# Loading v by token tiles, with GpSimd copies across the partition halves, in a fused attention and expert kernel

## The chip, the core and the metric

The program runs on one core of a Trainium2 chip. TensorE (PE in the rows; PEld is its weight load) multiplies, VectorE (DVE), ScalarE (ACT) and GpSimd (POOL) work on tiles of 128 partitions, and SyncE (SP) issues most of the DMAs. A row of an engine's name with a q (SPq, POOLq) is that engine's instruction queue. The metric is the device time of one execution in microseconds (us), as the median of several runs.

## The reference, cut to what matters

```python
q_c, k_c, v_c = (a.reshape(B, H, 9, 64, 64) for a in (q, k, v))   # B=8, H=8, S=576 tokens, D=64
scores = np.matmul(q_c, k_c.transpose(0, 1, 2, 4, 3)) / np.sqrt(64)
attn = np.exp(scores - scores.max(-1, keepdims=True))
attn = attn / (attn.sum(-1, keepdims=True) + 1e-09)
x = np.matmul(attn, v_c)               # per chunk of 64 tokens and head
x = x.reshape(B, H, S, D).transpose(0, 2, 1, 3).reshape(4608, 512)
# stage 2: tokens with x @ w_skip > 0 go to the best of 8 experts (512 -> 1024 -> 512), gated, plus x
# stage 3: h = max(x @ w1, x @ w2, x @ w3) (768 wide); out = h @ w_out
```

Attention is local: the 64 tokens of a chunk attend only to each other, in each of 8 heads. All numbers are float32.

## The kernel before, in words

The 4608 tokens are worked on in 36 tiles of 128 tokens, two chunks each. Two tiles form a unit of 256 tokens, for which q and k are loaded together (`load_qk`, L191 to L204), five units ahead of use. A row of 512 bytes holds two neighbouring tokens, so a pair copy (`pair_heads`, L213 to L219) first brings them into shape: on ScalarE for unit 0, on VectorE for unit 1, on GpSimd from unit 2 on. TensorE turns them (`qk_transpose`), ScalarE moves the result to SBUF (qT and kT, L234), and `scores` multiplies them in quarters of the array, 64 by 64: the quarter's rows are the half of the partitions in which a head lies (`par`, 0 or 1, even or odd head), its columns the half that stands for one of the two chunks (`c2`). VectorE takes the maximum and subtracts it (L251, L253), ScalarE takes the exponential, TensorE turns the result, ScalarE copies it to aT (L267), and `values` (L273 to L297) multiplies it with v. A column of ones behind the 64 columns of v gives the sum by which VectorE divides (L293 to L295).

For this product the rows of v must lie in the same half of the partitions as the head's rows of aT. Before, `load_v` (L206 to L211) brings one batch of 576 tokens with eight DMAs, one for each head, each to the 64 partitions of its head's half: token k of a chunk lies in partition k or 64 + k, and the chunks lie side by side. Three such tiles (NV = 3, L173 and L174) hold three batches. Batch 0 is loaded in two parts, behind units 1 and 2 of q and k; batches 1 and 2 follow units 3 and 4; a later batch is loaded when the product has left the one three before it (L586 to L588).

Behind the product come the routing steps: `x_transpose`, `logits`, and for each group of four tiles `route`, `place` and `store_x` (L440 to L445, GpSimd's DMA of 512 tokens to `x_dram`) and, nine tiles behind, `send_id` (L420 to L429, a GpSimd DMA for each tile). The first tile of a group also clears the last columns of the rows for its tokens (a memset on GpSimd, L291), in one of two buffers whose earlier rows must have been stored. From tile 22 on the weights of the first expert are loaded (`load_raw`, L94 to L98) behind the last load issued so far, and split by ScalarE (L90) and VectorE (L91).

The order of TensorE's instructions is that of the program text in this loop (L573 to L635). On the other engines, SP and the DMA queues among them, a planner orders the instructions by its own estimate of when each can run; the chip then runs each engine's instructions in that order. Where one waits, all behind it on that engine wait.

Of the kernel before, what the change touches and what calls it, by code (L numbers as in the profile page):

```python
# [9 lines left out]
F32 = mybir.dt.float32  # L10
# [9 lines left out]
P = 128  # L20
B, H, S, D = 8, 8, 576, 64
# [6 lines left out]
UT = 256  # L28
NU = N // UT
NT = N // P  # L30
# [7 lines left out]
def kernel(  # L38
# [15 lines left out]
    nc = tc.nc  # L54
# [16 lines left out]
    def four_kb(shape, dt, name, aside=False):  # L71
        return bpool.tile(shape, dt, tag="s4" if aside else "b4", name=name, bufs=2 if aside else 4)
# [93 lines left out]
    def two_banks(tag, name):  # L166
        return psum1.tile([P, 2, 512], F32, tag=tag, name=name)

    apool = p1.enter_context(tc.tile_pool(name="apool", bufs=2))
    nc.gpsimd.memset(ids_sb, N)  # L170
    nc.gpsimd.dma_start(ids_dram.rearrange("(p c) o -> p (c o)", p=P), ids_sb)

    NV, CB = 3, S // 64  # L173
    v_all = [apool.tile([P, CB, 4, D + 1], F32, name=f"v_all{i}", bufs=1) for i in range(NV)]  # L174
    for i, t in enumerate(v_all):
        (nc.gpsimd if i else nc.vector).memset(t[:, :, :, D], 1.0)
    none = kpool.tile([1, XW], F32, name="none")
    nc.gpsimd.memset(none, 0.0)
    nc.gpsimd.dma_start(x_dram[N:N + 1, :], none)

    def pieces(u):
        got, t = [], u * UT
        while t < (u + 1) * UT:
            b, s = divmod(t, S)
            n = min((u + 1) * UT - t, S - s)
            got.append((t - u * UT, b, s, n))
            t += n
        return got


    def load_qk(u):  # L191
        if u % 5 < 3:
            qt = four_kb([P, H, 2 * D], F32, f"qt{u}", u % 5 == 2)
            kt = four_kb([P, H, 2 * D], F32, f"kt{u}", u % 5 == 2)
        else:
            both = bpool.tile([P, 2, H, 2 * D], F32, tag="b8", name=f"qkt{u}")
            qt, kt = both[:, 0], both[:, 1]
        for h0, h1 in [(0, 4), (4, 8)] if u == 0 else [(0, 8)]:
            for off, b, s, n in pieces(u):
                pr = slice(off // 2, (off + n) // 2)  # L200
                for dst, src in ((qt, q), (kt, k)):
                    link["load"] = nc.sync.dma_start(
                        dst[pr, h0:h1], src[b, h0:h1, s:s + n, :].rearrange("h (p r) d -> p h (r d)", r=2))
        units[u] = {"qt": qt, "kt": kt}  # L204

    def load_v(b, c0=0, c1=CB):  # L206
        for h in range(H):
            rows = slice(64 * (h % 2), 64 * (h % 2) + 64)
            link["load"] = nc.sync.dma_start(
                v_all[b % NV][rows, c0:c1, h // 2, :D],  # L210
                v[b, h, 64 * c0:64 * c1, :].rearrange("(c k) d -> k c d", k=64))  # L211

    def pair_heads(u, g):  # L213
        un = units[u]
        for nm in ("q", "k"):
            r = apool.tile([P, 2, H // 2, D], F32, tag=nm + "r", name=f"{nm}r{u}_{g}", bufs=3)
            (nc.scalar.copy if u == 0 else nc.gpsimd.tensor_copy if u > 1 else nc.vector.tensor_copy)(
                r, un[nm + "t"][:, 4 * g:4 * g + 4, :].rearrange("p h (r d) -> p r h d", r=2))
            un[nm + "r", g] = r  # L219
# [47 lines left out]
        nc.scalar.copy(aT, tr)  # L267
        un["aT", s] = aT

    def v_of(chunk):  # L270
        return v_all[chunk // CB % NV][:, chunk % CB]

    def values(t):  # L273
        u, s = divmod(t, 2)
        un = units[u]
        xp = two_banks("xp", f"xp{t}")[:, :, :4 * (D + 1)].rearrange("p r (h d) -> p r h d", h=4)
        for hp in range(4):
            for par, c2 in TILES:
                rows, cols = slice(64 * par, 64 * par + 64), slice(64 * c2, 64 * c2 + 64)
                nc.tensor.matmul(  # L280
                    xp[cols, par, hp, :], un["aT", s][rows, hp, cols], v_of(2 * t + c2)[rows, hp, :],
                    start=True, stop=True)
        g, j = PLACE[t]
        if j == 0:
            if g == len(SIZES) - 1:
                parts = [four_kb([P, 1, XW], F32, f"xg{g}_{i}", True) for i in range(SIZES[g])]
            else:
                parts = [bpool.tile([P, GT, XW], F32, tag="xg", name=f"xg{g}")[:, :SIZES[g], :]]
            groups[g] = parts, apool.tile([P, GT, E + 1], F32, tag="lg", name=f"lg{g}")
            for part in parts:  # L290
                nc.gpsimd.memset(part[:, :, DM + 1:], 0.0)  # L291
        sm = apool.tile([P, 2, 4], F32, tag="sm", name=f"sm{t}", bufs=3)
        nc.vector.tensor_scalar_add(sm, xp[:, :, :, D], 1e-9)  # L293
        nc.vector.reciprocal(sm, sm)
        nc.vector.tensor_tensor(  # L295
            rows_of(t)[:, :DM].rearrange("p (h r d) -> p r h d", h=4, r=2), xp[:, :, :, :D],
            sm.unsqueeze(3).to_broadcast([P, 2, 4, D]), op=ALU.mult)  # L297

    def rows_of(t):
        g, j = PLACE[t]  # L300
        part, i = divmod(j, groups[g][0][0].shape[1])
        return groups[g][0][part][:, i, :]
# [240 lines left out]

    AHEAD = 11

    units, xt, groups, slots, picks, xgs, xT, link, put, sent = {}, {}, {}, {}, {}, {}, {}, {}, {}, []
    ids_rows = ids_dram.rearrange("(p c) o -> p (c o)", p=P)

    def in_turn(load, *what):
        with tc.issue_after(link["load"].ins) if "load" in link else nullcontext():  # L550
            load(*what)

    first_v = {1: [(0, 0, 4)], 2: [(0, 4, CB)], 3: [(1,)], 4: [(2,)]}
    def load_gates():
        nc.sync.dma_start(wcat[:, :, :E], w_gate.rearrange("(c p) e -> p c e", p=P))
        link["load"] = nc.sync.dma_start(wcat[:, :, E], w_skip.rearrange("(c p) -> p c", p=P))

    for u in range(5):
        in_turn(load_qk, u)
        for part in first_v.get(u, ()):  # L560
            in_turn(load_v, *part)
        if u == 2:
            in_turn(load_gates)
        if u < 2:
            pair_heads(u, 0)
            pair_heads(u, 1)
            if u == 0:
                qk_transpose(0, 0)
                qk_transpose(0, 1)
# [3 lines left out]
    for t in range(NT + LAG):  # L573
        u, s = divmod(t, 2)
        if s == 0 and u + 5 < NU:
            load_qk(u + 5)
        if u + 2 < NU:
            pair_heads(u + 2, s)
        if t == 8:
# [3 lines left out]
            nc.gpsimd.tensor_copy(col_f, col_i)  # L583
        if 0 <= t - 2 < NT:
            values(t - 2)
        done = (2 * t - 2) // CB - 1  # L586
        if done >= 0 and (2 * t - 4) // CB <= done and done + NV < B:
            load_v(done + NV)  # L588
        if t < NT:
            scores(t)  # L590
        if t % 2 == 0 and 0 <= t - 22 <= 16:
            i = (t - 22) // 2
# [18 lines left out]
        if 0 <= t - 4 < NT:  # L611
            g, j = PLACE[t - 4]
            if j + 1 == SIZES[g]:
# [10 lines left out]
                if g == FIRST:  # L624
# [3 lines left out]
                    rows = START[g + 1] * P  # L628
# [251 lines left out]
    rows = bpool.tile([P, 4, XW], F32, tag="xg", name="xg_0")  # L880
# [165 lines left out]
    for b, (r0, n) in enumerate(BLOCKS):  # L1046
# [31 lines left out]
        for half in range(2):  # L1078
            for i in range(n // P):
# [11 lines left out]
                r = r0 + half * n + i * P  # L1091
# [32 lines left out]
```

## Time and profile before

| | |
|---|---|
| median of 3 runs | 1116.15 us (1113.48 to 1120.66) |
| profiled execution | 1114.1 us |
| its span, from the first to the last instruction | 1112.4 us |
| mean granted TensorE clock | 0.958 of full speed |
| busy: PE, DVE, ACT, POOL | 92%, 51%, 37%, 31% of the span |
| DMA | 217.12 MB, 195 GB/s over the span |

The share of an engine's busy time is over the whole span; a stage can look different. Matmuls overlap each other, so a busy TensorE is not one at its peak. In a timeline row the first number is the start in us from the span's start, the second the time that the instruction (or a run of like ones, xN) took, and the brackets hold the idle time of the engine before it and what ended that. The share of the DMA engines is a mean over 16 engines and can exceed 1, as packets overlap.

### The profile page before, as it was taken

The page shows a single profiled execution, that of the slowest core. Times are in us where ns is not written, and L with a number is a line of the kernel's source. Part 1 is how long each engine was busy: PE and PEld are TensorE (multiplying, and loading weights), DVE is VectorE, ACT ScalarE, POOL GpSimd, SP SyncE. Part 2 cuts the span into 40 slices and gives each one's busy share as a digit, 9 for nine tenths or more (in the row PEclk, how much of TensorE's full clock was granted, in tenths as well). Part 3 has the DMA queues.
Part 4 walks back from the last instruction along what each step waited for, and adds up shares of the span by engine and source line. Part 5 has one row for each costly group of instructions (what it writes and reads, how often), then busy time and mean ns, then how long its engine had stood idle before and what let it go on. Part 6 is the DMA issues. An engine that isn't in the chain of part 4 may idle for free.

```text
span 1112.4 us, 19589 instructions
## 1 busy us (share of the span) xinstructions
PE 1023.5 (92%) x7544; PEld 870.5 (78%) x7544; DVE 570.7 (51%) x1113; ACT 416.5 (37%) x737; POOL 340.8 (31%) x339
## 2 busy tenths in 40 slices
PE   7778879888999997999899799999999999999997
PEld 5667768777878786887687588788888888788996
DVE  3566657666855477351498762335234442443241
ACT  4546557334434335341444242222322232223231
POOL 2254434372432244530432160122312140223021
PEclk8989969698999998999999899999999999999999
DMA  8999983366863548454998734664466545666591
GB/s 197 200 271 222 252 222 117 135 204 231 287 225 118 187 159 284 154 178 144 299 322 287 262 114 139 189 188 118 164 195 188 165 140 167 178 187 207 187 286 38
DMA packets 213616, 217.12 MB, mean 195 GB/s; under 512 B 48779, under 2 KB 177803, under 8 KB 213504
## 3 DMA queue, kind: packets, MB, share of 16 engines
q1 hardware_dynamic: 200320, 174.18, 55.2%
q0 software_dynamic: 10592, 33.20, 8.6%
q10 hardware_dynamic: 2592, 8.26, 2.0%
q8 instruction: 69, 1.13, 0.4%
q14 instruction: 43, 0.35, 0.1%
HBM read 175.15 MB, written 41.83 MB: 195 GB/s over the span
## 4 chain that ended last, share of the span: by engine, by line
PE 41%; DMA 6%; DVE 3%; issue 3%; POOL 1%; ACT 0%; SPq 0%; POOLq 0%; DVEq 0%; ACTq 0%
PE f_a L681 5%; PE f_a L683 5%; PE f_a L682 5%; PE o L681 4%; PE o L682 4%; PE o L683 4%; DMA ws<-m_sums 3%; PE f_d L681 3%; PE f_d L683 3%; PE f_d L682 3%; DMA m_sums<-n_q 2%; PE f_b L681 1%; PE f_b L682 1%; PE f_b L683 1%; PE trf L855 1%
## 5 line engine op out<-in xcount | busy, mean ns | idle before, releaser
L91 POOL TENSOR_TENSOR fh<-best,fh 128x512 fp32r<-128x512 f32 (+1 forms) x60 | 77.1, 1291 | 361.0 <-ACT fh L90 276.2
L681 PE MATMUL f_a<-x_t,ws 128*128 128x512 f32 (+1 forms) x270 | 100.8, 373 | 6.2 <-DVE p L1009 5.5
L682 PE MATMUL f_a<-x_t,ws 128*128 128x512 f32 (+1 forms) x270 | 99.9, 370 | 0.0
L683 PE MATMUL f_a<-x_t,ws 128*128 128x512 f32 (+1 forms) x270 | 99.7, 370 | 0.0
L90 ACT CAST whi_e<-raw_e 128x1024 fp32r<-128x1024 f32 x64 | 66.0, 1048 | 71.7 <-DMA raw_e<-in_moe_w_dram 40.8
L681 PE MATMUL h<-xhi,whi_e 128*128 128x256 f32 x256 | 76.2, 298 | 12.8 <-ACTq L958 7.0
L682 PE MATMUL o<-wlo_m,fh 128*128 128x512 f32 x216 | 84.6, 392 | 0.0
L681 PE MATMUL o<-whi_m,fh 128*128 128x512 f32 x216 | 83.4, 392 | 0.0
L683 PE MATMUL o<-whi_m,fh 128*128 128x512 f32 x216 | 83.4, 392 | 0.0
L682 PE MATMUL h<-xlo,whi_e 128*128 128x256 f32 x256 | 75.2, 294 | 0.1
L683 PE MATMUL h<-xhi,wlo_e 128*128 128x256 f32 x256 | 74.6, 293 | 0.0
L681 PE MATMUL y<-whi_e,hhi 128*128 128x512 f32 x184 | 73.9, 403 | 0.6 <-ACT hhi L748 0.6
L683 PE MATMUL y<-whi_e,hlo 128*128 128x512 f32 x184 | 72.9, 399 | 0.2
L682 PE MATMUL y<-wlo_e,hhi 128*128 128x512 f32 x184 | 72.4, 394 | 0.0
L91 POOL TENSOR_TENSOR wlo_e<-raw_e,whi_e 128x1024 fp32r<-128x1024 f32 x21 | 52.8, 2514 | 50.3 <-ACT whi_e L90 44.1
L90 ACT CAST fh<-best 128x512 fp32r<-128x512 f32 (+1 forms) x60 | 34.7, 579 | 88.6 <-DVE best L1011 57.0
L91 DVE TENSOR_TENSOR wlo_e<-raw_e,whi_e 128x1024 fp32r<-128x1024 f32 x43 | 53.4, 1256 | 27.5 <-ACT whi_e L90 26.2
L681 PEld LDWEIGHTS h<-xhi,whi_e 128*128 128x128 f32 x256 | 51.8, 203 | 15.9 <-ACTq L958 10.4
L681 PEld LDWEIGHTS f_a<-x_t,ws 128*128 128x128 f32 x270 | 51.1, 189 | 15.9 <-DVE p L1009 5.9
L1014 ACT COPY p<-f_a 128x512 f32<-128x512 f32 (+1 forms) x45 | 24.6, 546 | 99.1 <-PE f_a L683 98.9
L683 PEld LDWEIGHTS f_a<-x_t,ws 128*128 128x128 f32 x270 | 51.2, 190 | 8.6
L682 PEld LDWEIGHTS f_a<-x_t,ws 128*128 128x128 f32 x270 | 51.2, 190 | 8.3
(216 smaller groups left out, 2582.7 us busy)
## 6 DMA issues: line engine op xcount, KB each, us to landing
ws<-m_sums SPq DMA_DIRECT2D x135, 512.0 KB, 5.0
raw_e<-in_moe_w_dram SPq DMA_DIRECT2D x64, 512.0 KB, 4.1
ws<-m_sums SPq DMA_DIRECT2D x45, 256.0 KB, 3.9
x<-x_dram SPq DMA_DIRECT2D x36, 256.0 KB, 4.3
out_dram<-os SPq DMA_DIRECT2D x36, 256.0 KB, 2.0
x_dram<-xg POOLq DMA_DIRECT2D x8, 1040.0 KB, 6.9
v_all<-in_v_dram SPq DMA_DIRECT2D x56, 144.0 KB, 5.6
m_sums<-n_raw ACTq DMA_DIRECT2D x18, 448.0 KB, 4.8
```

The lines of the kernel that those rows point to most:

```text
L90: nc.scalar.copy(hi, src),
L91: eng.tensor_tensor(lo, src, hi.bitcast(F32), op=ALU.subtract),
L681: nc.tensor.matmul(acc, ahi, bhi, start=first, stop=False, skip_group_check=onto)
L682: nc.tensor.matmul(acc, ahi, blo, start=False, stop=False, skip_group_check=onto)
L683: return nc.tensor.matmul(acc, alo, bhi, start=False, stop=last, skip_group_check=onto)
L855: nc.tensor.transpose(tr[:, i * P:(i + 1) * P], row[:, c * P:(c + 1) * P], ident)
L1014: nc.scalar.copy(p1, acc_a)
```

## The change

v is loaded by the tile of 128 tokens, one token to a partition, with all eight heads side by side (one DMA, or two where the tile crosses the end of a batch). Eight such tiles are held; the first eight are loaded behind units 1 to 4 of q and k, two at a time, and the tile t + 6 in step t, once the product of tile t - 2 has run. In this layout chunk 0 of a tile lies in partitions 0 to 63 and chunk 1 in 64 to 127, for all heads; the quarters in which the head's half and the chunk's half differ (`par` not equal to `c2`) read v from another tile, `vm`, into which `cross` copies the even heads of the upper half and the odd heads of the lower half, two copies of 64 partitions by 4 x 65 elements for each tile. VectorE makes them for tiles 0 and 1, GpSimd for the others. The matmuls are the same in number and shape. The GpSimd DMA scratch has its default size again.

```diff
-    NV, CB = 3, S // 64
-    v_all = [apool.tile([P, CB, 4, D + 1], F32, name=f"v_all{i}", bufs=1) for i in range(NV)]
+    NV = 8
+    v_all = [apool.tile([P, H, D + 1], F32, name=f"v_all{i}", bufs=1) for i in range(NV)]
     for i, t in enumerate(v_all):
-        (nc.gpsimd if i else nc.vector).memset(t[:, :, :, D], 1.0)
+        (nc.gpsimd if i > 1 else nc.vector).memset(t[:, :, D], 1.0)
...
-    def pieces(u):
-        got, t = [], u * UT
-        while t < (u + 1) * UT:
+    def pieces(t, end):
+        got, t0 = [], t
+        while t < end:
...
-    def load_v(b, c0=0, c1=CB):
-        for h in range(H):
-            rows = slice(64 * (h % 2), 64 * (h % 2) + 64)
+    def load_v(t):
+        for off, b, s, n in pieces(t * P, (t + 1) * P):
             link["load"] = nc.sync.dma_start(
-                v_all[b % NV][rows, c0:c1, h // 2, :D],
-                v[b, h, 64 * c0:64 * c1, :].rearrange("(c k) d -> k c d", k=64))
+                v_all[t % NV][off:off + n, :, :D], v[b, :, s:s + n, :].rearrange("h k d -> k h d"))
+
+    def cross(t):
+        vn = v_all[t % NV].rearrange("p (h r) d -> p r h d", r=2)
+        vm[t] = apool.tile([P, H // 2, D + 1], F32, tag="vm", name=f"vm{t}", bufs=4)
+        eng = nc.vector if t < 2 else nc.gpsimd
+        for par in range(2):
+            to, of = slice(64 * par, 64 * par + 64), slice(64 - 64 * par, 128 - 64 * par)
+            eng.tensor_copy(vm[t][to], vn[of, par])
...
-    def v_of(chunk):
-        return v_all[chunk // CB % NV][:, chunk % CB]
+    def v_of(t, par, c2):
+        return v_all[t % NV].rearrange("p (h r) d -> p r h d", r=2)[:, par] if c2 == par else vm[t]
...
-                    xp[cols, par, hp, :], un["aT", s][rows, hp, cols], v_of(2 * t + c2)[rows, hp, :],
+                    xp[cols, par, hp, :], un["aT", s][rows, hp, cols], v_of(t, par, c2)[rows, hp, :],
...
-    first_v = {1: [(0, 0, 4)], 2: [(0, 4, CB)], 3: [(1,)], 4: [(2,)]}
+    first_v = {1: (0, 1), 2: (2, 3), 3: (4, 5), 4: (6, 7)}
...
         if s == 0 and u + 5 < NU:
             load_qk(u + 5)
+        if t < NT:
+            cross(t)
         if u + 2 < NU:
             pair_heads(u + 2, s)
...
-        done = (2 * t - 2) // CB - 1
-        if done >= 0 and (2 * t - 4) // CB <= done and done + NV < B:
-            load_v(done + NV)
+        if t >= 2 and t - 2 + NV < NT:
+            load_v(t - 2 + NV)
...
-    nc = _bacc.Bacc("TRN2", target_bir_lowering=False, num_devices=1, dynamic_dma_scratch_size=8192)
+    nc = _bacc.Bacc("TRN2", target_bir_lowering=False, num_devices=1)
```

## Rows read from the trace of the kernel before

**Rows 1.** The page, busy time (share of the span) and instructions.
```profile
PE 1023.5 (92%) x7544; PEld 870.5 (78%) x7544; DVE 570.7 (51%) x1113; ACT 416.5 (37%) x737; POOL 340.8 (31%) x339
```

**Rows 2.** Busy time by stretch: length; PE, PEld, DVE, ACT, POOL; clock, DMA share, GB/s.
```profile
60.00:76.00 16.00, 9.69 (x172) 8.83 (x162) 10.23 (x26) 6.16 (x15) 8.79 (x13) 0.79 1.13 275
76.00:136.00 60.00, 54.40 (x1196) 48.98 (x1198) 40.16 (x138) 36.12 (x80) 29.02 (x45) 1.00 1.17 242
136.00:156.00 20.00, 11.86 (x206) 10.82 (x199) 5.83 (x11) 7.87 (x14) 7.59 (x11) 0.66 1.12 252
```

**Rows 3.** Timeline of TensorE: starts of the value products (L280).
```profile
36.80 0.69 PE L280 MATMUL xp<-v_all,aT 64*64 64x65 f32 x30
...
50.37 0.70 PE L280 MATMUL xp<-v_all,aT 64*64 64x65 f32 x32
...
76.22 0.70 PE L280 MATMUL xp<-v_all,aT 64*64 64x65 f32 x32
...
135.38 0.70 PE L280 MATMUL xp<-v_all,aT 64*64 64x65 f32 x32
...
155.17 0.70 PE L280 MATMUL xp<-v_all,aT 64*64 64x65 f32 x32
```

**Rows 4.** TensorE's waits, 0 to 206 us: total, times, longest.
```profile
PE trp L264 <- ACT qT L234: 10.1, 6, 8.1
PE trx L308 <- DVE xg L295: 5.7, 1, 5.7
PE trq L232 <- POOL qr L217: 4.1, 2, 3.2
PE trk L232 <- POOL kr L217: 3.7, 4, 1.4
```

**Rows 5.** Timeline of SP's queue (DMA issues).
```profile
36.40 9.11 SPq L209 DMA_DIRECT2D v_all<-in_v_dram  x8
...
59.03 4.13 SPq L202 DMA_DIRECT2D qkt<-in_k_dram  x1
...
123.36 12.06 SPq L209 DMA_DIRECT2D v_all<-in_v_dram  x8
...
136.27 1.36 SPq L97 DMA_DIRECT2D raw_e<-in_moe_w_dram  x1
```

**Rows 6.** Timeline of GpSimd, TensorE and ScalarE: first work behind a late load.
```profile
42.39 1.17 POOL L217 COPY qr<-qkt 128x512 f32<-128x512 f32 x2 [9.94 <-DMA qkt<-in_q_dram]
...
54.83 0.66 PE L232 MATMUL trk<-ident,kr 128*128 128x128 f32 x4 [1.01 <-POOL kr L217]
...
143.00 1.04 ACT L90 CAST whi_e<-raw_e 128x1024 fp32r<-128x1024 f32 x1 [7.45 <-DMA raw_e<-in_moe_w_dram]
```

**Rows 7.** DMA queue of SP, 39 to 45 us: packets, MB, share.
```profile
q1 hardware_dynamic: 3581, 1.08, 126.3%
```

**Rows 8.** Pair copies by shape on VectorE and GpSimd: busy us, mean ns | idle before.
```profile
L217 DVE COPY qr<-qt 128x512 f32<-128x512 f32 x2 | 0.8, 424 | 3.2 <-DMA qt<-in_q_dram 3.2
...
L217 POOL COPY qr<-qt 128x512 f32<-128x512 f32 x20 | 12.5, 630 | 36.2 <-DMA qt<-in_q_dram 23.7 <-issue 6.9 <-PE trq L232 4.6
```

**Rows 9.** Timeline of GpSimd: id sends, pair copies, a store and a memset.
```profile
61.99 0.99 POOL L422 DMA_INDIRECT ids_dram<-tok_i,rslot  x1 [0.30 <-PE sc L247]
63.29 0.98 POOL L422 DMA_INDIRECT ids_dram<-tok_i,rslot  x1 [0.30 <-PE lp L316]
...
65.54 0.63 POOL L217 COPY qr<-qt 128x512 f32<-128x512 f32 x1
...
68.32 0.60 POOL L217 COPY kr<-kt 128x512 f32<-128x512 f32 x1
...
127.73 0.81 POOL L444 DMA_DIRECT2D x_dram<-xg  x1 [1.48 <-DVE run L352]
134.81 0.12 POOL L291 MEMSET xg<- 128x28 f32 x1 [6.27 <-DMA x_dram<-xg]
```

**Rows 10.** Timeline of VectorE: adds of routing.
```profile
65.58 3.37 DVE L352 TENSOR_TENSOR run<-run,roh 128x8 bf16<-128x8 bf16 x2
```

More of the change, by code (lines that the diff above doesn't have):

```diff
@@ L179 @@
     nc.gpsimd.dma_start(x_dram[N:N + 1, :], none)
-    def pieces(u):
-        got, t = [], u * UT
-        while t < (u + 1) * UT:
+    def pieces(t, end):
+        got, t0 = [], t
+        while t < end:
             b, s = divmod(t, S)
-            n = min((u + 1) * UT - t, S - s)
-            got.append((t - u * UT, b, s, n))
+            n = min(end - t, S - s)
+            got.append((t - t0, b, s, n))
             t += n
@@ L198, in load_qk @@
         for h0, h1 in [(0, 4), (4, 8)] if u == 0 else [(0, 8)]:
-            for off, b, s, n in pieces(u):
+            for off, b, s, n in pieces(u * UT, (u + 1) * UT):
                 pr = slice(off // 2, (off + n) // 2)
@@ L544 @@
     AHEAD = 11
-    units, xt, groups, slots, picks, xgs, xT, link, put, sent = {}, {}, {}, {}, {}, {}, {}, {}, {}, []
+    vm, units, xt, groups, slots, picks, xgs, xT, link, put, sent = {}, {}, {}, {}, {}, {}, {}, {}, {}, {}, []
     ids_rows = ids_dram.rearrange("(p c) o -> p (c o)", p=P)
@@ L560 @@
         for part in first_v.get(u, ()):
-            in_turn(load_v, *part)
+            in_turn(load_v, part)
         if u == 2:
```

## The prediction

> **What bounds the kernel now.** I began with busy time per engine: TensorE is busy 92% of the span [rows 1]. So the time is TensorE's work plus the places where it waits, and the change adds and removes no TensorE instruction. It touches the attention stage alone, roughly the first 204 us. I cut that stage into stretches [rows 2]. From 76 to 136 us TensorE is busy 54.4 of 60 us at a granted clock of 1.00; from 60 to 76 it is busy 9.7 of 16 at 0.79, from 136 to 156 11.9 of 20 at 0.66. The reader is to see two holes here, after each of which the clock falls to between its levels, so that the next tile also runs slower.
>
> The undisturbed pace comes from the starts of the value products [rows 3]: 76.22 to 135.38 us holds 14 tiles, 4.23 us a tile. At that pace two tiles take 8.5 us. From 36.80 to 50.37 two tiles took 13.6 us, 5.1 too many; from 135.38 to 155.17 two took 19.8, 11.3 too many.
>
> Next, what TensorE waited for [rows 4]: 10.1 us for ScalarE's qT, of which one wait is 8.1; 5.7 in one wait for VectorE's xg; 4.1 and 3.7 for the pair copies on GpSimd (longest 3.2 and 1.4). Two of these four lead back to the load queue. SP holds eight v DMAs in a row: 9.11 us at 36.40, 12.06 at 123.36 [rows 5]. Behind the first, the q of unit 4 reached GpSimd only at 42.39, after a 9.94 us wait for its DMA; lateness of the same kind cost TensorE the 1.4 us [rows 4] and 1.01 at 54.83 [rows 6]. Behind the second, the first expert weight was issued only at 136.27 [rows 5], ScalarE stood 7.45 us at its cast [rows 6], and the qT copy queued behind that cast is the 8.1 us wait.
>
> **The change, part by part.**
>
> *Load queue.* 72 v DMAs become 40 (36 tiles; four straddle a batch and need two pieces). Bytes and the 256-byte run stay. With v alone in flight 3,581 packets took 126% of the engines' 6 us [rows 7]; I take that cost per packet as unchanged, so what changes is order: before unit 4's q and k come 1.6 MB of v (six tiles) instead of 2.4 MB (two batches). At 1.08 MB in 6 us [rows 7] the 0.8 MB are 4.4 us, more than the 3.2 us wait. I take the whole 5.1 us excess at 36.80, the 1.4 and the 1.0, and 0.9 of the other 2.2 us of waits for pair copies (7.8 less 3.2, 1.4 and 1.0). The SP cost of one 256 KB v DMA isn't shown: below, 9.11/8 = 1.1 us, above, the 4.13 us of a blocked 512 KB k load [rows 5]; either way SP is never held for 9 to 12 us on end. The load of v for tile t+6 now waits for the product of tile t-2 and for its copies; queued behind it are q, k and the weights, which are needed 8 tiles later or in the MoE stage, and so can bear it.
>
> *First weight.* It is issued after the last v load. That is now one 256 KB DMA instead of eight, so the 12.06 us hold shrinks to about 1 to 4, against a 7.45 us wait. Bounds: nothing gained, or the 11.3 us excess. I take 11.3, since 12.06 less 4.13 is 7.9 and covers the wait. Gains together: 5.1 + 2.4 + 0.9 + 11.3 = 19.7 us.
>
> *VectorE copies of tiles 0 and 1.* Four of 64 x 260. A 128 x 512 copy on VectorE is 0.424 us [rows 8]; by elements per partition 0.22, so 0.9 us in the chain to the first product, with nothing to hide it. Bounds 0 and 1.7 (four full copies); I take 0.9, nearer in shape. More memsets at the start (eight small ones for three) lie beside GpSimd's first wait and I cost them at nothing; without that cover, eight of 0.12 us [rows 9] would be 1.0.
>
> *GpSimd copies of tiles 2 to 35.* 68 of 64 x 260, a form the trace doesn't have, as they also move data to the other 64 partitions. Below: 0.12 us of a memset [rows 9] plus 260/512 of what a 128 x 512 copy takes beyond that, 0.63 - 0.12 [rows 8], gives 0.38. Above: 0.63, a whole copy. I take 0.38, since these copies are the same operation on half as many elements: 3.0 us per four tiles, 26 us in all. Is there room? Per four tiles, 16.9 us, GpSimd is busy 8.2 (29.0 of 60 us [rows 2]). Id sends start 1.30 us apart but last 0.99 [rows 9], adding 1.2 for four. And its queue stands from 128.54 to 134.81 at the memset of the next token rows, which waits 6.27 us for the store of the earlier rows [rows 9]. That is 15.7 of 16.9; with 3.0 more it is 18.7, too much by 1.8 unless copies run inside that wait. They need only v (loaded six tiles ahead) and one of four buffers, so those planned ahead of the memset are hidden; those behind it are what a value product would wait for. I take half hidden and 2 us in all; bounds 0, and with the upper price (5.0 per four tiles, 3.8 too much, six times) 23.
>
> *VectorE beside GpSimd.* At 65.58 two adds of routing took 3.37 us for eight elements a partition each, ending as a run of six GpSimd copies, from 65.54 to 68.92, ran out [rows 9, 10]; xg behind them gave the 5.7 us wait. So an add with both inputs in SBUF stood through the run, not through one copy. Longer runs make this likelier: I take one more, 5.7 us. Bounds: the present one goes (-5.7), or four more (23). The Trainium skill, "SBUF — State Buffer", section "Who interferes with whom", says that such an instruction and a GpSimd instruction that reads SBUF exclude each other until the one that issued first finishes. By that rule alone each collision would cost one copy, 0.6 us, and the sum would be 5 us better; the row shows five times that, and it decides.
>
> *Descriptor scratch.* The kernel's GpSimd DMA scratch goes back to its default. No row shows a DMA issue waiting for it; I cost it at nothing.
>
> **Sum.** -19.7 + 0.9 + 2 + 5.7 = -11.1 us in the attention stage. The MoE stages follow in TensorE's order and start when the routing ends, so I pass it on whole; a planner that orders the later stages otherwise is why the forecast's own range is 6 us either way, a width that I choose. The profiled execution is 1114.1 us (span 1112.4 and 1.7 around it), so 1103.0; the median of the runs is 2.05 higher, hence 1105.0.
>
> **Rivals.**
>
> *GpSimd becomes the bound (slower).* Place: the copies behind the memset that waits for the store. Price: 3.8 us per four tiles over six groups, 23, and two further collisions, 11.4. It decides once GpSimd's work per four tiles passes 16.9 us, which 1.2 us more already does if none of it fits inside the 6.27 us wait. -19.7 + 0.9 + 23 + 11.4 = +15.6: 1132. For it: 15.7 of 16.9 is already taken. Against: the pair copies run several buffers ahead and the wait itself is idle time.
>
> *Copies are free (better).* All of them fall into that wait, and runs get shorter because q and k no longer arrive in a heap: -19.7 + 0.9 = -18.8, 1097; with the present collision gone too, 1092. For it: the burst at 65.54 had queued up behind late loads and id sends. Against: id sends stay, and hold GpSimd 5.2 us at a time.
>
> *The change doesn't reach the late weight.* Packets are as many and as small, so the weight may land as late, and the planner may put the cast as early as before. Then only 8.4 of the 19.7 us come back, and 8.6 are lost: 1116, no change. For it: the DMA share from 76 to 156 us is 1.12 to 1.17 [rows 2], near the 1.26 with v alone [rows 7]. Against: the 12.06 us that SP spent before that weight.
>
> **How the numbers follow.** About 1% (11 us) is what a measurement can tell from no change. Chances: forecast 0.45 (1099 to 1111, its middle on that line), copies free 0.15, weight still late 0.18, GpSimd the bound 0.22. Faster by over 1%: 0.25 of the forecast, 0.15, and 0.02 of the third, 0.42. Slower: 0.18 of the last and 0.03 of the third, 0.21. Within 1%: the remaining 0.37. The range leaves out a tenth at each end: down to 1093, just above copies free with the collision gone, and up to 1130, most of the way to the slower case. The faster cases alone run from 1092 to 1105.
>
> **What would show it.** Right: no stretch of SP beyond 4 us on v; no wait for unit 4's q near 40 us; ScalarE's first weight cast without a wait of several us and the granted clock near 1.00 from 136 to 156; GpSimd copies of 0.3 to 0.4 us. Wrong: value products waiting for the copies, routing adds of several us in more than two places, GpSimd copies above 0.6 us, or a hole of the same length in the MoE stage, which would mean that the gain was given back there.

## The result, and the profile after

The changed kernel took 1132.7 us, the median of four runs, against 1118.41 for four runs of the kernel before beside it: ratio 1.013, 95% interval 1.0086 to 1.0174. It is slower by 14.3 us, where 1105 had been forecast. In two of the five sets of runs below the kernel before took 1136 us, at a lower granted clock, instead of 1115 to 1118, so every ratio in this document is to the kernel before in the same set. The profiled execution has a span of 1128.7 us, 16.3 more than before. The last value product starts at 225.1 us instead of 204.3, so the attention stage ends 20.8 us later, and what follows is 4.5 us shorter (903.6 instead of 908.1).

Line numbers are five or six higher than before. TensorE's stretches, with the columns of [rows 2]:

```profile
17.00:60.00 43.00, 39.46 (x809) 35.84 (x811) 27.15 (x82) 28.25 (x59) 20.50 (x39) 0.96 1.15 229
60.00:76.00 16.00, 13.07 (x266) 11.62 (x260) 9.68 (x25) 8.67 (x18) 7.58 (x15) 0.95 1.02 236
76.00:136.00 60.00, 44.28 (x795) 40.90 (x795) 26.65 (x89) 25.49 (x53) 28.73 (x50) 0.78 0.90 208
136.00:156.00 20.00, 18.14 (x341) 15.98 (x340) 13.27 (x43) 12.10 (x24) 12.12 (x22) 0.83 0.72 199
156.00:204.00 48.00, 34.61 (x573) 30.40 (x575) 27.06 (x86) 23.91 (x48) 30.33 (x50) 0.79 0.46 143
```

Against [rows 2] the holes moved. From 60 to 76 us TensorE is busy 13.07 us instead of 9.69, and from 136 to 156 it is 18.14 instead of 11.86, as the prediction had it. But from 76 to 136, where nothing was to be lost, 54.40 us at a clock of 1.00 became 44.28 at 0.78. Counted in value products, the changed kernel was ahead at 75 us (12.4 tiles of 36 against 10.5) and behind at 135 (21.4 against 23.5) and 195 (30.8 against 34.5). These counts by window come out a half to one and a quarter tiles high by the end of the stage, so differences below a tile are not to be read.

What TensorE waited for, 0 to 230 us (total, times, longest):

```profile
PE trx L313 <- DVE xg L300: 13.0, 4, 6.9
PE trq L237 <- POOL qr L222: 10.7, 5, 4.3
```

The 8.1 us for qT of [rows 4] is gone; the waits for GpSimd's pair copies (4.1 us before) and for VectorE's xg (5.7) have more than doubled. Both lead to GpSimd: xg stood for stores of token rows that GpSimd issues, which it did nowhere before,

```profile
DVE xg L300 <- DMA x_dram<-xg: 14.9, 5, 4.4
```

and TensorE's longest single wait for xg, 6.9 us, is explained below. GpSimd's copies, all of them, with what its queue stood for ahead of them:

```profile
L216 POOL COPY vm<-v_all x68: 394/399/787, 21.2 to 208.6; 64x260 f32<-64x260 f32 x68
its engine sat idle before it (us, times) until:
  DMA ids_dram<-tok_i,rslot: 29.9, 10
  PE trx L313: 14.2, 3
  PE xp L285: 7.8, 2
```

A copy takes 399 ns (the median), as costed. Yet the queue stands 29.9 us, in ten places, until the DMAs of id sends have landed, which have nothing to do with v. It stands a further 31.3 us ahead of copies for TensorE (the two rows above and 4.6, 3.9 and 0.8 us more). In the program, the one thing of TensorE's that a copy waits for is the product of the tile four before, which frees one of the four buffers of `vm`; as TensorE itself was late, part of this is an effect of the loss. A timeline of GpSimd shows how a wait for a send comes about (the bracket is the idle time ahead):

```profile
156.00 1.00 POOL L427 DMA_INDIRECT ids_dram<-tok_i,rslot  x1 [0.16 <-issue]
161.43 0.90 POOL L216 COPY vm<-v_all 64x260 f32<-64x260 f32 x2 [4.43 <-DMA ids_dram<-tok_i,rslot]
162.48 0.99 POOL L427 DMA_INDIRECT ids_dram<-tok_i,rslot  x1 [0.15 <-POOL vm L216]
163.52 0.61 POOL L222 COPY qr<-qkt 128x512 f32<-128x512 f32 x1
```

A send is issued at 156.00, the next copy starts 4.43 us after the send's end, and the next send and the pair copies queue behind it. It is in the compiled program, in GpSimd's order of instructions with the semaphores that each waits for (the sends of lines 65 and 67 count up DMASW3 and DMASW4):

```
65 L427 DMA ids_dram<-tok_i,rslot_890 36864x1 [waits DMASW0_49,DVE_49,Pool_49]
66 L216 COPY vm_1075<-v_all_132 64x260
67 L427 DMA ids_dram<-tok_i,rslot_890 36864x1
...
70 L216 COPY vm_1193<-v_all_133 64x260 [waits DMASW4_49,DMASW3_49,DMAHW0_49,PE_49,Pool_49]
```

18 of the 68 copies wait like this. In the kernel before no copy waits for a send, and the four sends of a group stand one behind the other; here most of them are spread one or two at a time between copies. Late sends have one more customer. VectorE computes the first expert's row numbers ("at") when the sent ids can be loaded:

```profile
174.80 0.69 DVE L258 TENSOR_TENSOR ex<-sc,mx 128x512 f32<-128x512 f32 x1
185.10 0.66 DVE L636 TENSOR_SCALAR at<-ids 128x2 int32<-128x2 int32 x1 [9.61 <-DMA ids<-ids_dram]
185.61 0.15 DVE L298 TENSOR_SCALAR sm<-xp 128x8 f32<-128x8 f32 x1
...
186.95 1.09 PE L313 MATMUL trx<-ident,xg 128*128 128x128 f32 x4 [6.85 <-DVE xg L300]
```

Before, this instruction stood 1.44 us and ran at 172.61, at the same place in VectorE's order. Here it stands 9.61 us with a tile's normalization (sm, xg) behind it. TensorE waits 6.85 us for that xg and is busy 3.12 of the 10 us from 180 to 190 (9.67 before):

```profile
180.00:190.00 10.00, 3.12 (x69) 2.53 (x68) 3.09 (x7) 1.84 (x4) 7.57 (x13) 0.68 0.04 6
```

### The profile page after: what moved, and what is told of

Same layout as the page of the kernel before. It is cut to its first block, busy times and chain, and to the rows that moved or that the text cites. A ratio compares the mean times of both kernels' runs of the same rounds, so it can differ in the third digit from the quotient of the medians.

```text
span 1128.7 us, 19653 instructions
## 1 busy us (share of the span) xinstructions
PE 1032.5 (91%) x7544; PEld 879.0 (78%) x7544; DVE 570.0 (51%) x1118; ACT 418.7 (37%) x737; POOL 363.8 (32%) x411
## 4 chain that ended last, share of the span: by engine, by line
PE 44%; DMA 5%; DVE 1%; issue 0%; ACT 0%; SPq 0%; ACTq 0%; DVEq 0%
PE f_a L687 6%; PE f_a L689 6%; PE f_a L688 6%; PE o L687 4%; PE o L689 4%; PE o L688 4%; DMA ws<-m_sums 4%; PE f_d L687 3%; PE f_d L688 3%; PE f_d L689 3%; PE f_b L689 1%; PE f_b L688 1%; PE f_b L687 1%; PE trf L861 1%; DMA m_sums<-n_q 1%
## 5 line engine op out<-in xcount | busy, mean ns | idle before, releaser
L91 DVE TENSOR_TENSOR wlo_e<-raw_e,whi_e 128x1024 fp32r<-128x1024 f32 x43 | 55.8, 1313 | 23.4 <-ACT whi_e L90 21.4
L687 PEld LDWEIGHTS f_a<-x_t,ws 128*128 128x128 f32 x270 | 51.1, 189 | 16.5 <-DVE p L1015 5.9
L678 POOL DMA_INDIRECT x_dram<-xg,ids_sb x20 | 20.8, 1039 | 115.3 <-DVEq L902 46.9
L689 PEld LDWEIGHTS f_a<-x_t,ws 128*128 128x128 f32 x270 | 51.2, 190 | 8.6
```

The costliest lines, as they stand in the source:

```text
L91: eng.tensor_tensor(lo, src, hi.bitcast(F32), op=ALU.subtract),
L678: ins = nc.gpsimd.indirect_dma_start(out=x_dram[:, :], out_offset=bass.IndirectOffsetOnAxis(ap=ids, axis=0), in_=xg, in_offset=None, bound ...
L687: nc.tensor.matmul(acc, ahi, bhi, start=first, stop=False, skip_group_check=onto)
L689: return nc.tensor.matmul(acc, alo, bhi, start=False, stop=last, skip_group_check=onto)
```

## The experiments

The theories: **A**, the copies' wait for id sends is the loss; **B**, GpSimd's added work is, 68 times 0.40 us; **C**, the new loads cost the time. All medians are in us. A set is a group of runs taken together with the kernel before; there were five. The ratio is to the kernel before in the same set, with its 95% interval, and ratios are compared within a set first. The last two columns are starts, in us, in the profiled execution: of the last value product and of the instruction for "at".

One thing has to be kept in mind where two runs differ by copies: the planner arranges the whole program anew. In the compiled programs of the changed kernel and e1 or e16, of e1 and e2 or e3, of e5 and e6, of e6 and e7, and of the kernel before and e4, the order of the other instructions on VectorE, ScalarE and GpSimd differs too. In e4's, for example, "at" stands behind the softmax of tile 28 and not, as in the kernel before, behind that of tile 29. The difference between two such runs is therefore the price of the copies together with that of the new order, and no run separates these two.

| run | set | median | ratio | interval | last value product | "at" |
|---|---|---|---|---|---|---|
| before (profile of the first run) | | 1118.41 | | | 204.3 | 172.6 |
| changed | | 1132.7 | 1.013 | 1.009 to 1.017 | 225.1 | 185.1 |
| e1 VectorE copies | 1 | 1111.85 | 0.996 | 0.994 to 0.998 | 209.5 | 168.1 |
| e2 same + spare GpSimd copies | 1 | 1126.41 | 1.007 | 1.005 to 1.009 | 221.4 | 175.1 |
| e3 one half each | 1 | 1116.64 | 0.999 | 0.997 to 1.001 | 209.2 | 165.5 |
| e4 before + spare copies | 1 | 1125.03 | 1.006 | 1.004 to 1.008 | 222.0 | 177.3 |
| e5 new order, old layout | 2 | 1124.65 | 1.010 | 1.006 to 1.014 | 218.9 | 180.3 |
| e6 same + spare copies, no id wait | 2 | 1132.01 | 1.016 | 1.012 to 1.020 | 223.0 | 184.8 |
| e7 same, with id wait | 2 | 1156.29 | 1.037 | 1.033 to 1.042 | 252.2 | 208.7 |
| e8 e5 + old scratch size | 2 | 1129.16 | 1.012 | 1.009 to 1.016 | 223.7 | 182.5 |
| e9 before + early weights | 3 | 1138.44 | 1.001 | 0.998 to 1.005 | 223.0 | 185.3 |
| e10 e5 + early weights | 3 | 1122.73 | 0.988 | 0.982 to 0.993 | 221.6 | 178.0 |
| e11 e1, copies later | 3 | 1130.57 | 0.996 | 0.993 to 1.000 | 217.8 | 173.1 |
| e12 e3, copies later | 3 | 1136.87 | 1.000 | 0.997 to 1.004 | 232.9 | 186.2 |
| e13 e10 again | 4 | 1117.98 | 1.002 | 1.000 to 1.004 | 216.7 | 177.5 |
| e14 before, one execution | 4 | 1110.61 | | | 203.5 | 173.5 |
| e15 e9, one execution | 4 | 1115.9 | | | 201.6 | 168.6 |
| e16 ScalarE copies | 4 | 1111.57 | 0.996 | 0.994 to 0.999 | 205.0 | 165.8 |
| e17 changed, "at" on GpSimd | 5 | 1133.69 | 1.000 | 0.996 to 1.004 | 228.4 | 194.6 |
| e18 e16, "at" on GpSimd | 5 | 1126.06 | 0.992 | 0.989 to 0.996 | 216.4 | 174.4 |

**e1, all copies on VectorE.**

```
-        eng = nc.vector if t < 2 else nc.gpsimd
+        eng = nc.vector
```

> The changed kernel with all 72 copies on VectorE (0.291 us each there, against 0.399 us on GpSimd), and nothing else edited. Theory A, the wait: in the changed kernel's program the first copy of a token tile stands on GpSimd until the id sends ahead of it have landed (29.9 us of such waits in the trace, 5.2 the longest), and pair copies, stores and sends queue behind it; VectorE's copies carry no such wait. Then the gains of the new load order stay and little is lost: 1100 us (1094 to 1108), the last value product near 190 us (204.3 before, 225.1 after), no wait of GpSimd for ids_dram. Rival B, too much work on GpSimd: the 68 copies times 0.40 are 27 us of GpSimd's queue; this also gives about 1100 here, and is told apart by the next run. Rival C, the new v loads themselves cost the time: still 1125 to 1135, with the last value product near 225.

No copy waits for an id send now, and the loss is gone; but 1111.85 is only 5 us below the kernel before, not 17. VectorE's busy time shows the price there (count | busy us, mean ns | idle ahead):

```profile
L216 DVE COPY vm<-v_all 64x260 f32<-64x260 f32 x68 | 23.5, 346 | 31.9 <-PE xp L285 15.3 <-DMA v_all<-in_v_dram 13.7 <-issue 1.3
```

23.5 us of work in the 68 copies of this stretch, and VectorE stands 31.9 us ahead of the copies with the softmax of later tiles behind. C, as put (1125 or more), is out.

**e2, the same, and GpSimd as busy as in the changed kernel.** The spare tile is read by nothing.

```
             eng.tensor_copy(vm[t][to], vn[of, par])
+            if t > 1:
+                nc.gpsimd.tensor_copy(spare[t % 2][to], vn[:64, 1])
```

> The kernel with the copies on VectorE, and beside them GpSimd also makes 68 copies of the same 64 x 260 shape from the same v tiles into a spare tile that nothing reads. They wait for the v loads, and not for any id send. Theory A (the wait): GpSimd is as busy as in the changed kernel, yet the time stays within 5 us of the run with VectorE copies alone, 1100 to 1105. Rival B (GpSimd's work): back to 1120 to 1135, with TensorE waiting for pair copies as in the changed kernel (10.7 us). Rival C: 1125 to 1135.

A fell as the whole story: without any wait for an id send, 68 copies of 407 ns on average cost 14.6 us over e1. They are not quite free of waits, though: they stood 8.3 us for v loads.

**e3, half of the copies left on GpSimd**, those that read partitions 0 to 63 and wait for no send.

```
-        for par in range(2):
-            ...
-            eng.tensor_copy(vm[t][to], vn[of, par])
+        nc.vector.tensor_copy(vm[t][:64], vn[64:, 0])
+        eng.tensor_copy(vm[t][64:], vn[:64, 1])
```

> Of each tile's two copies only the one that reads partitions 0 to 63 stays on GpSimd (34 copies), which in the program waits for no id send; the other one goes to VectorE. Theory A: all of the wait is gone, 1098 to 1106, as with VectorE copies alone. Rival B: half of GpSimd's extra work is left, so about half of the loss, 1112 to 1120. Rival C: 1125 to 1135.

1116.64, 4.8 over e1: B's side, and none of GpSimd's copies waits for a send in this program.

**e4, the kernel before with 68 spare copies.**

```
+        if 2 <= t < NT:
+            nc.gpsimd.tensor_copy(tick[t % 2][:64], big[:64, :260])
+            nc.gpsimd.tensor_copy(tick[t % 2][64:], big[:64, :260])
```

> The kernel before, its v loads untouched, with 68 spare copies of 64 x 260 on GpSimd, two per token tile, from a constant tile into a tile that nothing reads; none waits for an id send or a load. Theory A: 68 x 0.40 = 27 us of work that mostly finds GpSimd idle, 1116 to 1121. Rival B: GpSimd has no room for 27 us more, 1126 or above, and the memset behind the store and the pair copies come later. The prediction's own term for these copies alone was 2 us, with 23 as its upper bound.

7.7 us: nearer to B, well above the prediction's 2. These are the only spare copies that wait for nothing. How the work turns into time is only partly seen. The copies ran between 4 and 118 us, but the tiles fell behind after 150 (24.1 done by then against 24.5 in e14's trace of the kernel before, 31.1 against 34.0 by 195), where VectorE stood 6.3 us for the row numbers (now a tile earlier in its order), ScalarE 5.7 for the weight, and the clock was low. So no copy stood in GpSimd's way when the time was lost, and the new order may hold part of the 7.7. e4's stretches:

```profile
170.00:180.00 10.00, 8.18 (x108) 7.58 (x107) 3.56 (x8) 4.60 (x8) 4.81 (x6) 0.77 0.05 7
180.00:190.00 10.00, 8.72 (x143) 7.85 (x144) 6.59 (x22) 6.38 (x13) 5.09 (x8) 0.57 0.38 124
```

and the same of e14:

```profile
170.00:180.00 10.00, 8.80 (x182) 7.88 (x182) 8.17 (x29) 7.17 (x15) 5.18 (x9) 1.00 0.35 109
180.00:190.00 10.00, 9.70 (x183) 9.00 (x183) 7.30 (x19) 6.74 (x13) 6.06 (x7) 0.83 0.45 161
```

TensorE is busy nearly as long and does 251 matmuls instead of 365, at a granted clock of 0.77 and 0.57 instead of 1.00 and 0.83: part of the loss appears as a low clock, whatever brought it down.

**e5, the load order without copies**, v in the layout of the kernel before.

```
+        for c in range(2):
+            b, s = divmod(t * P + 64 * c, S)
+            for par in range(2):
+                link["load"] = nc.sync.dma_start(
+                    v_all[t % NV][64 * par:64 * par + 64, c, :, :D],
+                    v[b, par::2, s:s + 64, :].rearrange("h k d -> k h d"))
...
```

> The load order of the changed kernel without its copies: v still comes one tile of 128 tokens at a time into eight tiles, but each head's 64-token chunk goes straight to the half of the partitions where the products want it, as in the kernel before (four DMAs of 64 KB for a tile in place of one of 256 KB). No copy is left on any engine. Theory L1: the load order is worth what the prediction summed for it, 19.7 us, so 1094 to 1102 and a last value product near 188 us. Rival L2: it is worth little more than the VectorE version showed (1111.9), because a tile of attention still takes TensorE and its producers about 5 us (three tiles in 15 us there, whatever the holes): 1104 to 1112, last value product after 195. Rival L3: the load order itself is worth nothing, 1114 to 1120.

Outside all three: 1124.65, slower than before. At first it runs ahead (22.0 tiles by 120 us against 20.5), then TensorE is busy 2.61 of the 20 us from 136 to 156. SP's and ScalarE's timelines:

```profile
143.03 3.53 SPq L209 DMA_DIRECT2D v_all<-in_v_dram  x4
146.61 0.59 SPq L97 DMA_DIRECT2D raw_e<-in_moe_w_dram  x1
...
151.77 1.04 ACT L90 CAST whi_e<-raw_e 128x1024 fp32r<-128x1024 f32 x1 [21.57 <-DMA raw_e<-in_moe_w_dram]
```

Four 64 KB v DMAs hold SP 3.53 us; 144 of them stand in the queue with everything else, and the first weight is issued ten microseconds later than before. This layout doesn't price the load order alone.

**e6 and e7, e5 with 68 spare GpSimd copies**, from partitions 0 to 63 (no id wait) or across, as in the changed kernel (nine wait for sends).

```
+        if 1 < t < NT:
+            for par in range(2):
+                to, of = slice(64 * par, 64 * par + 64), slice(0, 64)
+                nc.gpsimd.tensor_copy(spare[t % 4][to], v_all[t % NV][of, par])
```

In e7 "of" is slice(64 - 64 * par, 128 - 64 * par).

> The run above, plus 68 copies of 64 x 260 on GpSimd from the v tiles into a spare tile that nothing reads, all from partitions 0 to 63, so that none waits for an id send in the program. Theory A, as revised by the first four runs (GpSimd's added work is the larger part of the loss): 8 to 15 us above the run above, as 68 such copies cost 7.7 us in the kernel before and 14.5 beside VectorE's. Rival (only the waits cost): within 3 us of it.

> The same 68 spare copies, now from the other half of the partitions as in the changed kernel; in the program nine of them wait for id sends that stand just ahead. Theory: the waits add to the work, another 4 to 8 us over the run with copies from partitions 0 to 63, and stores come late (VectorE's xg waits for a store by 10 us or more in all). Rival: within 2 us of it, the waits are idle time.

e6: 7.4 us over e5, as much as in e4. But its copies stood a long time for v loads (GpSimd's waits, 17 to 260 us), and TensorE stood 22.5 us for the pair copies behind them, so this is not the price of the work alone:

```profile
POOL spare L582 <- DMA v_all<-in_v_dram: 44.4, 17, 5.6
```

e7: 24.3 over e6, far more than expected. The same waits in e7:

```profile
POOL spare L582 <- DMA v_all<-in_v_dram: 34.2, 10, 7.4
POOL xg L293 <- DMA x_dram<-xg: 24.3, 4, 8.9
POOL spare L582 <- DMA ids_dram<-tok_i,rslot: 14.9, 7, 3.8
```

The wait for sends is 14.9 us itself and puts the sends and stores behind it later still: the row numbers run at 208.65 instead of 184.81, and the memset of token rows (xg L293) stands 24.3 us for stores (3.9 in e6). The copies stood less for v than in e6, so v doesn't explain it. A is a part, then, and B as well (e2, e4).

**e8, the DMA scratch of the kernel before in e5.**

```
-    nc = _bacc.Bacc("TRN2", target_bir_lowering=False, num_devices=1)
+    nc = _bacc.Bacc("TRN2", target_bir_lowering=False, num_devices=1, dynamic_dma_scratch_size=8192)
```

> The load order without copies, and with the DMA scratch at 8192 bytes a partition as in the kernel before, where the change left the default. The prediction costed that at nothing: within 2 us of the first run of this set. If the larger scratch lets GpSimd's DMAs go earlier, this run is slower by more than that.

4.5 us slower by the medians, with ratios whose intervals overlap. The larger scratch of the change doesn't cost; whether it saves something isn't settled.

**e9, the largest gain alone: the weights' loads four tiles earlier.**

```
-        if t % 2 == 0 and 0 <= t - 22 <= 16:
+        if t % 2 == 0 and 0 <= t - 18 <= 20:
             i = (t - 22) // 2
             with tc.issue_after(link["max"].ins), tc.issue_after(link["exp"].ins):
-                if i < 8:
-                    with tc.issue_after(link["load"].ins):
-                        raws_0[i] = load_raw(*expert_src(0, i))
-                if i:
+                if i > 0:
                     expert_piece(0, i - 1, wpool, raw=raws_0[i - 1])
+                if i + 2 < 8:
+                    with tc.issue_after(link["load"].ins):
+                        raws_0[i + 2] = load_raw(*expert_src(0, i + 2))
```

> The kernel before, its v loads untouched, with the loads of the first expert's weights issued four tiles earlier (two loads further ahead of their casts), so that they stand ahead of the last two v batches in SP's queue. This tries the largest gain of the prediction by itself: 11.3 us for the first weight coming in time. Theory G (the gain is real and keeps): ScalarE's 7.45 us wait for the weight is gone, TensorE's busy time from 136 to 156 us rises from 11.9 to 17 or more, and the time falls to 1102 to 1108. Rival H (given back): the hole goes, but the tiles behind it run no sooner, because the v and q behind the weights come later by the same bytes: 1112 to 1118.

ScalarE no longer waits for the weight, and the ratio is 1.001: the rival.

**e10, the same in e5, and e13, e10 again.**

> The run with v tile by tile in the old layout and no copies (1124.65 us; there the 144 v DMAs took SP 0.88 us each, the first weight was issued only at 146.61 and ScalarE stood 21.57 us for it), with the weights issued earlier in the same way. Theory: that wait is what made this version slow; without it 1100 to 1108, and the load order's gain is shown free of copies. Rival: SP's issue time of the 144 DMAs holds back the q and k loads as well, 1115 or more.

> The version with v tile by tile in the old layout, no copies and the weights issued earlier, once more (ratio 0.988, interval 0.982 to 0.993, on a chip on which the kernel before took 1136 us). If its gain is real and not that chip's, the ratio is 0.983 to 0.993 again; otherwise above 0.995.

0.988 in the third set, 1.002 in the fourth: the gain did not repeat, and in e13's profile ScalarE again stood 8.01 us for the weight. Why one set showed it stays open.

**e14 and e15, the kernel before and e9, one execution of each.**

> The kernel before, unchanged, for a trace from the same chip as the next run. Expected as before: a hole of TensorE of 7 us or more between 136 and 156 us, where ScalarE waits for the first weight, and a last value product near 204 us.

> The kernel before with the weights issued earlier (ratio 1.001, interval 0.998 to 1.005), for a trace from the same chip. It says where the 11.3 us went. Theory H1 (the loads set the pace up to 156 us): no hole at the weight, but no more tiles done by 150 us than in the run of the kernel before, since the DMA engines are as full in both; last value product within 3 us of it. Rival H2: the last value product comes 8 us earlier or more, and the gain is lost behind it, in the start of the expert stage.

e14 settles more than it was meant to. ScalarE's first weight in this execution of the unchanged kernel:

```profile
144.16 1.04 ACT L90 CAST whi_e<-raw_e 128x1024 fp32r<-128x1024 f32 x1 [2.35 <-DMA raw_e<-in_moe_w_dram]
```

and its stretch around it:

```profile
136.00:156.00 20.00, 17.50 (x273) 16.30 (x271) 9.27 (x22) 9.63 (x19) 9.12 (x12) 0.72 1.12 239
```

The wait is 2.35 us, not the 7.45 of [rows 6], TensorE is busy 17.50 us, not 11.86, and still the last value product comes at 203.5 instead of 204.3. This execution stood a tile behind at 135 us (22.5 against 23.5) and level at 150 (24.5 in both): ScalarE's cast starts at nearly the same time, 143.00 and 144.16, and only how long the engines stand ahead of it differs. The hole on which 11.3 us of the prediction rested is there in one execution and hardly in the next, and the tiles end at the same time. e15, with no wait at all: 201.6, within H1's 3 us, though a tile ahead at 150 us (25.5), which H1 had not expected, and no gain in the time.

**e11 and e12, e1 and e3 with the copies one tile later**, just ahead of their products.

```
-        if t < NT:
-            cross(t)
...
+        if 0 <= t - 1 < NT:
+            cross(t - 1)
         if 0 <= t - 2 < NT:
             values(t - 2)
```

> The VectorE version (1111.85 us), each tile's copies put one tile later in the program, just ahead of the products that need them. In that version VectorE's copies stood 15.3 us for TensorE's products to free their buffer and 13.7 us for v, in front of the softmax of later tiles. Theory V (VectorE's queue held the tiles at 5.0 us each): those waits shrink to under 10 us together, 1100 to 1107. Rival: the copies' own 23.5 us on VectorE are the price, and the products now wait for them: 1109 to 1115.

> The version with one half on GpSimd and one on VectorE (1116.64 us), also one tile later. Theory V: 1100 to 1110. Rival (GpSimd's 34 copies cost by their work, 5 us or more over VectorE alone): above the run before it by 4 to 6 us.

Ratios as without the move (0.996 and 1.000), the result that the rivals had named. But V isn't refuted by it: in e11 VectorE's copies still stood 20.0 us for the products and 11.0 for v, so the waits that the move was to shorten were as long as in e1.

**e16, all copies on ScalarE.**

```
-        eng = nc.vector if t < 2 else nc.gpsimd
+        eng = nc.scalar
...
-            eng.tensor_copy(vm[t][to], vn[of, par])
+            eng.copy(vm[t][to], vn[of, par])
```

> The changed kernel with all 72 copies on ScalarE. As with VectorE's (ratio 0.996), no copy waits for an id send and GpSimd has no more to do than before. ScalarE is busy 36 of 60 us from 76 to 136 us in the kernel before; 24 more tiles' copies at about 0.35 us each add 8 or so. Theory (any engine but GpSimd gives a small gain): ratio 0.990 to 1.000. Rival (ScalarE's queue feeds TensorE's transposes, qT and kT, so its copies cost more than VectorE's): 1.000 to 1.015.

0.996, as VectorE's. 410 ns each, 27.9 us for the 68 of this stretch:

```profile
L216 ACT COPY vm<-v_all 64x260 f32<-64x260 f32 x68 | 27.9, 410 | 18.3 <-DMA v_all<-in_v_dram 14.5 <-PE xp L285 2.8
```

So the same loads and copies gain 0.4% from two engines and lose 1.3% from GpSimd.

**e17 and e18, the row numbers on GpSimd** in the changed kernel and in e16.

```
-                    nc.vector.tensor_single_scalar(at, ids_0[:, :2], rows - 1, op=ALU.min)
+                    nc.gpsimd.tensor_single_scalar(at, ids_0[:, :2], rows - 1, op=ALU.min)
```

> The changed kernel with one small instruction moved: the minimum over the first expert's row numbers (128 x 2 integers), for which VectorE stood 9.61 us in the changed kernel and 1.44 in the one before, runs on GpSimd, whose gathers are the only ones to use it. Theory D (the late id sends cost mainly by that stand: VectorE's queue with the softmax of the next tile behind it, TensorE busy 3.12 of 10 us from 180 to 190): 7 to 10 us less than the changed kernel, ratio 1.003 to 1.007, and no 9 us wait on VectorE. Rival P (GpSimd's late copies hold every tile, the stand is one among many): ratio 1.010 to 1.017.

> The ScalarE version (ratio 0.996; VectorE stood 5.17 us for the row numbers there) with the same move. Theory D: 3 to 5 us less, ratio 0.991 to 0.995, the best version so far. Rival P: 0.995 to 1.000, as pair copies on GpSimd now queue behind that wait.

The ratios went D's way: 1.000 (better than D's range) against 1.013, 0.992 against 0.996. But both were compared across sets, and e10 and e13 show that one version's ratio can differ by that much between sets. e17's trace doesn't support D either: the last value product is at 228.4, no earlier than in the changed kernel (in another set), and GpSimd still stands for sends ahead of the copies:

```profile
POOL vm L216 <- DMA ids_dram<-tok_i,rslot: 32.5, 9, 5.4
POOL vm L216 <- DMA v_all<-in_v_dram: 10.9, 5, 6.0
```

What VectorE's stand is worth stays open. Within the fifth set, e18 is 7.6 us below e17: GpSimd is the wrong engine for the copies there too. e1, e16 and e18 are the versions whose intervals lie below the kernel before, by less than 1%; e10 did once, and not when repeated.

## Why the prediction was wrong

- **The failed step is "They need only v (loaded six tiles ahead) and one of four buffers ... I take half hidden and 2 us in all."** The copy's price was right (0.38 forecast, 0.399 measured). What they need was wrong: 18 of 68 also wait for id sends, 29.9 us in all, a wait that no term of the sum has. The wait for one of the four buffers is named and priced at nothing; the copies stood 31.3 us for TensorE to free one. And the hiding was wrong: copies that wait for nothing cost 7.7 us (e4), and those that wait only for v cost 14.6 (e2). With the same loads, the copies on ScalarE instead of GpSimd are 1.7% better (e16), some 19 us, so their place on GpSimd is what made the change slower. How the 19 us divide into the work, the waits for sends and those for buffers isn't shown: the work costs 7.7 to 14.6 us in other kernels, sends to wait for came with 24.3 us in e7, and no run changed the number of buffers.
- **The rival had the total by luck, not the mechanism.** "GpSimd becomes the bound" said 1132, with the copies behind the memset that waits for the store and two further collisions. In the changed kernel no memset stands like that; the copies themselves stand, for sends. And the price was set against 19.7 us of gains that weren't there.
- **The gains, 19.7, were mis-sized.** With the copies on VectorE or ScalarE the whole change gains 4 to 5 us (e1, e16), the copies' own cost there included. *First weight, 11.3:* its wait is gone in the changed kernel (ScalarE's cast at 148.74 follows without one) and brings nothing (e9, e14, e15). One execution's hole was taken for a constant. *Unit 4, 5.1:* q reaches GpSimd at 35.37 after 3.31 us of waiting, instead of 42.39 after 9.94, and the tiles are ahead at 75 us in the changed kernel and in e5; the lead is lost later. In e1 and e16 there is no lead at 75 us (10.5 tiles, as before). A hole early in a stage that goes on with loads in flight was priced as if the tiles behind it kept their 4.23 us; from 60 to 195 us e1, in which TensorE has no single wait of over 3.5 us for another engine, took 5.2 us a tile (26 tiles in 135 us), no less than the kernel before with its holes (25.9 tiles).
- *VectorE beside GpSimd, +5.7:* no collision was added, and the present one went, the term's lower bound: the adds of routing took at most 0.62 us in the changed kernel (2.82 before). What that gave isn't separated. Nor are two inputs in SBUF needed for it, as the prediction reads the row: in e14, beside the same run of six GpSimd copies, an instruction with one tensor input stood:

```profile
65.57 2.94 DVE L335 TENSOR_SCALAR rsm<-rsm 128x4 f32<-128x4 f32 x1
```

- *Copies of tiles 0 and 1, 0.9:* four of 0.291 us, 1.2. *Scratch, 0:* no loss (e8).
- *The clock* did not fall to between its levels behind the two holes: in the trace before it is 0.50, the lower one, from 70 to 73 and from 139 to 152 us; the 0.79 and 0.66 of [rows 2] are means over longer stretches.
- *"What would show it":* the first weight's cast and the copies' 0.4 us came out as "right" had it, unit 4's q nearly, and no value product waited for a copy; SP still stood 9.18 us on two v loads at 107.17, and the clock was 0.83 and not near 1.00 from 136 to 156. None of the marks was on the end of the stage, nor on what GpSimd's queue stood for.

## What to carry to other kernels

Before work is given to an engine with room by its busy share, list what else stands in its queue and read the compiled order for the semaphores of the new instructions: a wait for an unrelated DMA can come with them, and everything behind it pays. A hole is a cost only if it shows in a second execution and the end of the stage moves when it is taken away by itself: one small run of the unchanged kernel, and one that removes only that wait, would have taken 11 us out of this sum. A spare copy that nothing reads prices an engine's work only if it waits for nothing and leaves the other engines' order as it was.

## What the runs showed of the hardware

- A 64 x 260 f32 copy to the other half of the partitions took 399 ns on GpSimd (median; 407 on average), 291 on VectorE (four copies; 346 on average for 68 in e1) and 410 on ScalarE (e16).
- Which copies wait for id sends follows no rule that the runs settle. In the programs of these kernels it was GpSimd copies that read partitions 64 to 127 of a v tile, and neither those that read 0 to 63 nor any on VectorE or ScalarE. The Trainium skill, "GPSIMD Engine Reference", section "Instruction dispatch", says that a GpSimd instruction that reads partitions which another of its cores wrote in the instruction before needs a semaphore wait between them. No run here shows that rule at work: waits on GpSimd's own semaphore (Pool), as in the order above, stand ahead of 52 of the 64 pair copies in the kernel before too, which move nothing across partitions, and the waits for landed DMAs are of another kind.
- SP was held 3.53 us by four v DMAs of 64 partitions (64 KB each) in e5. In the changed kernel one of 128 partitions (256 KB) held it 0.37 us where it stood alone, and two in a row as long as 9.18, so how much of either is the issue itself isn't settled. The Trainium skill, "DMA: Bandwidth & Descriptors", section "Issuing engines are not separate DMA queues", calls the time to initiate a DMA usually small beside the DMA. In e5, where a weight's load stood in the same queue behind 64 KB pieces, ScalarE waited 21.57 us for that weight (7.45 before), and no run shows how much of it is time to initiate.
